# ScalarE takes apart and joins the 16-bit planes of the last four experts' tokens, in place of GpSimd

## The chip, the cores and the metric

The kernel runs on one core of one Trainium2 chip. The metric is the device time of one execution in microseconds (us), of that one core; the times shown are medians over several executions. A core has five engines that run side by side, each through its own queue in order: TensorE (PE in the profile, with its weight loads as PEld), VectorE (DVE), ScalarE (ACT), GpSimd (POOL) and SyncE (SP), which here issues DMAs. An engine waits at the head of its queue until the data of its next instruction are there, and everything behind that instruction waits too.

## The reference, cut to what matters

```python
def _attn_ref(q, k, v):                      # 8 batches, 8 heads, 576 positions, 64 wide
    scores = q @ k^T / 8 + slope[h] * -|i-j|, masked to 0 <= i-j < 128
    return softmax(scores) @ v

def _moe_ref(x, w_gate, w1, w2):             # x: 4608 tokens x 512; 8 experts, 1024 wide
    logits = x @ w_gate                      # 4608 x 8
    cap = 576                                # tokens that one expert may take
    # all (token, expert) pairs in falling order of logit: a token goes to the first
    # expert that still has room
    for e in range(8):
        mask = assigned == e                 # 576 tokens
        out[mask] = relu(x[mask] @ w1[e]) @ w2[e]
```

The output of the attention, as 4608 tokens of 512 float32 numbers, is the input `x` of the mixture of experts. Each of the eight experts gets exactly 576 tokens.

## The kernel before

The first third of the time is the attention (up to about 240 us), which writes `x` to a buffer in HBM and the gate logits to SBUF. It is not touched. Then come the experts, one after the other, in the order in which they fill up. **Round k** (k = 0 to 7) is the work on the k-th expert.

**One round** has two layers. Layer 1 (`layer1`) multiplies the 576 tokens by `w1`: eight blocks f of 128 hidden columns, each 24 matmuls of 288 tokens (192 in all) into two PSUM banks `ph`. ScalarE takes the ReLU out of each bank into `hh` (L1064) and VectorE the remainder into `hlo` (L1069). `ph` has four banks, so that block f+2 needs the banks of block f emptied. Layer 2 (`layer2`) multiplies the result by `w2`: five tiles t of 128 tokens (the last 64), 24 matmuls of 512 columns each for t = 0 to 3 and 16 for t = 4 (112 in all), each tile in one bank `po` out of two. ScalarE copies the bank to `o` (L1094), and GpSimd sends the rows to their places in the output with an indirect DMA (L1099). Float32 operands are used as a sum of two parts, a high part that the matmul takes as it is and a low part that holds the rest; three of the four products are summed. So weights are loaded from HBM by SyncE as `raw` (L958, four buffers), split by ScalarE into the high part of `hl` (L965) and by VectorE into the low part (L967, two instructions each). The tokens' parts are `xh` and `xl`.

**Preparing the next expert's tokens.** During round k the tokens of expert k+1 are gathered by five indirect DMAs (L976, GpSimd, 128 tokens each, the last 64) into `g`, and have to be turned so that the 512 features lie along the partitions. For the experts 1 to 3 TensorE turns them (`turn`). For the experts 4 to 7, that is in the rounds 3 to 6 (`BY_DMA = 3`), a DMA does (`turn_by_dma`), and a DMA transposes only 16-bit elements. So for each of the five tiles:

1. take apart: two copies put the upper and the lower 16 bits of each float32 of `g` into two planes `pl` (L1017);
2. SyncE asks for a transposing DMA from `pl` to `tp` (L1022), behind the loads of that round's weights;
3. join: two copies put the planes of `tp` back as the halves of float32 numbers in `xf` (L1029);
4. ScalarE copies `xf` to `xh` (L1037), and VectorE subtracts to `xl` (L1038).

`g`, `pl`, `tp` and `xf` share a ring of seven buffers (tag `g`), so a tile waits until an earlier one of the ring has been read. In the kernel before, GpSimd does the copies of steps 1 and 3: 20 copies in a round.

**The router** (`Router.phase`) finds the next experts on VectorE in many small instructions, with small matmuls between them on TensorE. Phase p yields the index list of expert p; it runs two rounds ahead, so that phase 5 runs in round 3, phase 6 in round 4 and phase 7 over the rounds 4 and 5. Its last step is a group of 18 matmuls into `m` (L817) that read `loOH` and `mv` (L812, L808, L809). `yield n` in a phase means that it goes on n slots later.

**What sets the order.** `layer1` yields twice per block f and `layer2` three times per tile t, so a round has 31 slots: 0 to 15 in layer 1, 16 to 30 in layer 2. After each, `slot(k, i)` traces what is due: router steps, weight loads (`W_LOAD`), weight splits (`W_SPLIT`), and the steps of the turning (`DMA_AT`: entry n is the slot from which step n is traced). This gives the order of tracing; a scheduler at build time then sets the order on each engine by its own estimate of when operands are ready, so an instruction may stand earlier on an engine that it thinks free. `add_manual_dep(a, b, BEHIND, ...)` puts a behind b in that order and adds no wait.

## Time and profile before

| | us |
|---|---|
| median of three runs (lowest, highest) | 692.59 (692.06, 695.39) |
| the profiled execution's own time | 690.85 |
| its span from first to last instruction | 688.9 |
| attention and the first routing | up to about 240.7 |
| rounds 0, 1, 2 | 240.7 to 416.0 |
| round 3, layer 1 / layer 2 from | 416.0 / 443.8 |
| round 4, layer 1 / layer 2 from | 471.2 / 498.3 |
| round 5, layer 1 / layer 2 from | 526.5 / 553.1 |
| round 6, layer 1 / layer 2 from | 579.5 / 605.1 |
| round 7, layer 1 / layer 2 from | 630.5 / 656.1 |
| last matmul | 681.9 |

Over the span TensorE is busy 95%, VectorE 70%, ScalarE 48%, GpSimd 28%. In a row of instructions of the profile stand the start, the duration, the engine, the line of the kernel, the operation, `out<-in`, the shape, a count, and in square brackets how long the engine sat idle before it and who ended that. A busy TensorE is not yet one at its peak, because matmuls overlap: the distance from one start to the next tells more than the duration.

### The profile page before, as it was taken

The numbers are of one execution on the slowest core, as the hardware profiler recorded it, in microseconds if no ns is written. First come the engines' busy times: TensorE is split into PE (matmuls) and PEld (weight loads), VectorE is DVE, ScalarE is ACT, GpSimd is POOL, SyncE is SP. The second block draws the span as 40 slices with busy tenths as digits, with TensorE's granted clock in tenths as the row PEclk, the third lists the DMA queues.
The fourth block names the chain that finished last, engine by engine and source line by source line (L and its number), as shares of the span: only waits on it lengthen the run. The fifth ranks groups of instructions, "written<-read, shape, count | busy, mean of one in ns | idle before, by whom it ended". The sixth has DMA issues, their size and how long they took to land.

```text
span 688.9 us, 18916 instructions
## 1 busy us (share of the span) xinstructions
PE 657.4 (95%) x7171; PEld 582.2 (85%) x7172; DVE 479.1 (70%) x1985; ACT 332.1 (48%) x991; POOL 192.7 (28%) x376
## 2 busy tenths in 40 slices
PE   7999999999995699999999999999989999999995
PEld 4898998998985399889789779979978978988985
DVE  5788888888887899879669788886775734532310
ACT  6898888888884262334134224324323333432210
POOL 4021221211220301511422017255076075152011
PEclk9999999999997799999999999999999999999998
DMA  8456566566532453615417227635625644621001
GB/s 307 148 181 202 175 193 200 166 211 186 161 106 70 124 191 104 241 39 187 158 36 245 88 92 245 131 106 182 133 98 166 167 111 169 160 52 54 1 25 49
DMA packets 54212, 97.47 MB, mean 141 GB/s; under 512 B 22880, under 2 KB 32224, under 8 KB 54112
## 3 DMA queue, kind: packets, MB, share of 16 engines
q1 hardware_dynamic: 48224, 77.30, 37.0%
q0 software_dynamic: 5888, 18.88, 8.3%
q8 instruction: 58, 0.95, 0.6%
q14 instruction: 42, 0.34, 0.1%
HBM read 72.57 MB, written 18.87 MB: 133 GB/s over the span
## 4 chain that ended last, share of the span: by engine, by line
PE 77%; DVE 12%; DMA 6%; issue 2%; ACT 1%; SPq 1%; POOL 0%; POOLq 0%; DVEq 0%; ACTq 0%
PE ph L1059 20%; PE po L1087 9%; PE po L1088 9%; PE s L54 8%; PE pt L54 7%; PE pt L158 7%; PE po L1090 7%; PE x L54 6%; DMA raw<-in_w_dram 2%; DVE hl L967 2%; DMA tp<-pl 1%; DVE hlo L1069 1%; DMA craw<-in_cst_dram 1%; PE pg L1000 1%; DMA qk<-in_qk_dram 1%
## 5 line engine op out<-in xcount | busy, mean ns | idle before, releaser
L1059 PE MATMUL ph<-xh,hl 128*128 128x288 f32 (+2 forms) x1024 | 188.9, 299 | 0.7 <-DVE lo L534 0.5
L1059 PEld LDWEIGHTS ph<-xh,hl 128*128 128x128 f32 x1024 | 154.7, 189 | 2.4 <-ACT hh L1064 1.0
L145 ACT ACTIVATE u<-u,mn 128x192 f32<-128x192 f32 (+2 forms) x288 | 123.9, 433 | 24.6 <-DVE mn L134 24.5
L1087 PE MATMUL po<-hl,hh 128*128 128x512 f32 (+1 forms) x328 | 128.9, 393 | 0.6 <-ACT o L1094 0.6
L1088 PE MATMUL po<-hl,hh 128*128 128x512 f32 (+1 forms) x328 | 126.4, 385 | 0.0
L967 DVE TENSOR_TENSOR hl<-raw,hl 128x512 fp32r<-128x512 f32 x128 | 88.1, 708 | 48.6 <-ACT hl L965 48.1
L1059 PE MATMUL ph<-xl,hl 128*128 128x288 f32 (+2 forms) x512 | 115.1, 297 | 0.0
L1064 ACT ACTIVATE hh<-ph 128x288 fp32r<-128x288 f32 (+2 forms) x128 | 46.6, 408 | 131.9 <-PE ph L1059 128.8
L134 DVE CUSTOM_DVE_ANT_0 u<-s,bm 128x192 f32<-128x192 f32 x308 | 86.5, 333 | 29.8 <-PE s L54 29.2
L1090 PE MATMUL po<-hl,hlo 128*128 128x512 f32 (+1 forms) x264 | 101.3, 384 | 0.0
L1099 POOL DMA_INDIRECT out_dram<-o,idx x40 | 42.5, 1063 | 153.1 <-ACT o L1094 76.0
L1059 PEld LDWEIGHTS ph<-xl,hl 128*128 128x128 f32 x512 | 84.1, 189 | 0.0
L965 ACT CAST hl<-raw 128x1024 fp32r<-128x1024 f32 x64 | 65.8, 1050 | 25.1 <-DMA raw<-in_w_dram 22.0
L1069 DVE SCALAR_TENSOR_TENSOR hlo<-ph,hh 128x288 fp32r<-128x288 f32 (+2 forms) x128 | 49.4, 417 | 35.8 <-ACT hh L1064 35.1
L1087 PEld LDWEIGHTS po<-hl,hh 128*128 128x128 f32 x328 | 61.8, 188 | 12.3 <-ACT o L1094 1.0
L54 PE MATMUL s<-qk 64*64 64x192 f32 (+1 forms) x1112 | 69.6, 319 | 2.5 <-DVE mn L134 1.8
L1088 PEld LDWEIGHTS po<-hl,hh 128*128 128x128 f32 x328 | 61.8, 188 | 11.0
L1094 ACT COPY o<-po 128x512 f32<-128x512 f32 (+1 forms) x33 | 18.8, 572 | 95.7 <-PE po L1090 77.4
L976 POOL DMA_INDIRECT g<-x,idx x40 | 42.1, 1053 | 72.2 <-issue 31.7
L1090 PEld LDWEIGHTS po<-hl,hlo 128*128 128x128 f32 x264 | 49.6, 188 | 10.0
L158 PE MATMUL pt<-ident_sb,u 128*128 128x128 f32 x368 | 54.2, 282 | 1.4 <-DVE mn L134 1.0
L54 PEld LDWEIGHTS s<-qk 64*64 64x64 f32 x1112 | 48.3, 132 | 8.3 <-issue 2.2
(240 smaller groups left out, 925.8 us busy)
## 6 DMA issues: line engine op xcount, KB each, us to landing
raw<-in_w_dram SPq DMA_DIRECT2D x64, 512.0 KB, 4.4
qk<-in_qk_dram SPq DMA_DIRECT2D x32, 576.0 KB, 4.8
v<-in_v_dram SPq DMA_DIRECT2D x32, 288.0 KB, 3.8
x<-xb SPq DMA_DIRECT2D x14, 512.0 KB, 3.5
x<-xb SPq DMA_DIRECT2D x8, 128.0 KB, 3.3
x<-xb SPq DMA_DIRECT2D x4, 256.0 KB, 2.4
g<-x,idx POOLq DMA_INDIRECT x40, 3.9
out_dram<-o,idx POOLq DMA_INDIRECT x40, 3.2
```

The lines of the kernel that those rows point to most:

```text
L54: put(nc.tensor.matmul(out, w, a, start=start, stop=stop, skip_group_check=True))
L134: put(nc.vector.tensor_tensor_reduce(out=u[rows], in0=x[rows, c:c + 64 * m].rearrange("q (j k) -> q j k", k=64), in1=bm[n % NP][rows, y:y ...
L145: put(nc.scalar.activation(u, u, AF.Exp, bias=st["mn"][:, i:i + 1], scale=-1.0, accum_out=st["sm"][:, i:i + 1]))
L158: put(nc.tensor.transpose(ps[:, c:c + 128], u[:, o + 128 * j:o + 128 * j + 128], ident))
L965: self.last = nc.scalar.copy(hl[:, 0, :], raw)
L967: nc.vector.tensor_tensor(hl[:, 1, c:c + 512], raw[:, c:c + 512], hl[:, 0, c:c + 512].bitcast(F32), ALU.subtract)
L1059: nc.tensor.matmul(pp[t], w[:, a, j, fo:fo + 128], x[:, j, cut[t]:cut[t + 1]], start=(i == 0), stop=(i == 11))
L1064: nc.scalar.activation(o, pp[t], AF.Relu)
L1069: nc.vector.scalar_tensor_tensor(d, pp[t][:, c0:c1], 0.0, o[:, c0:c1].bitcast(F32), ALU.max, ALU.subtract)
L1087: nc.tensor.matmul(out, a, wh, start=(f == 0), stop=False)
L1088: nc.tensor.matmul(out, a, wl, start=False, stop=(f == 7 and t == 4))
L1090: nc.tensor.matmul(out, hl[:, f, 128 * t:128 * t + 128], wh, start=False, stop=(f == 7))
```

## The change

ScalarE does the copies of the steps 1 and 3, 20 in each of the rounds 3 to 6. Two things go with it. The copies are put behind the last layer activation (`self.acted`: the last ReLU, or the last copy of `o`) in the order of ScalarE, and the table `DMA_AT` is new: the steps 1 are due in slots 4 to 8, the transposes in slot 9, and the steps 3, now together with step 4 for each tile, in slots 18, 20, 22, 24 and 26 (the key 2 of the table is not used, since `BY_DMA` stays 3). And the last wait of the router's phases 4 to 7 is one slot longer, as that of the phases 1 to 3 already was. `k > BY_DMA` in the router becomes `k > 3`, which is the same.

```diff
 BY_DMA = 3
-DMA_AT = [0, 1, 1, 2, 2, 2, 7, 7, 7, 7, 7, 9, 9, 10, 10, 10, 17, 19, 21, 23, 25]
+DMA_AT = {2: [10, 11, 11, 12, 12, 12, 13, 13, 13, 13, 13, 23, 24, 25, 26, 27], 3: [0, 4, 5, 6, 7, 8, 9, 9, 9, 9, 9, 18, 20, 22, 24, 26]}
...
-        yield WAITS[6] + (k < 4)
+        yield WAITS[6] + 1
...
+    def behind(self, copy):
+        self.tc.add_manual_dep(copy.ins, self.acted.ins.name, BEHIND, reason="layers first")
+
     def turn_by_dma(self, idx, asked):
...
             for a in range(2):
-                nc.gpsimd.tensor_copy(pl[:r, a, :], words[:r, :, 1 - a])
+                self.behind(nc.scalar.copy(pl[:r, a, :], words[:r, :, 1 - a]))
...
-        for tp, r in tps:
+        xh = self.p["xg"].tile([128, 4, CAP], F32R, name="xh")
+        xl = self.p["xg"].tile([128, 4, CAP], F32R, name="xl")
+        self.xg = xh, xl
+        for h, (tp, r) in enumerate(tps):
             xf = ring.tile([128, 4, 128], F32, name="xf", tag="g")
             words = xf.rearrange("q j t -> q (j t)").bitcast(U16).rearrange("q (j t o) -> q j t o", j=4, o=2)
             for a in range(2):
-                nc.gpsimd.tensor_copy(words[:, :, :r, 1 - a], tp[:, 4 * a:4 * a + 4, :r])
-            xfs.append((xf, r))
-            yield
-        xh = self.p["xg"].tile([128, 4, CAP], F32R, name="xh")
-        xl = self.p["xg"].tile([128, 4, CAP], F32R, name="xl")
-        self.xg = xh, xl
-        for h, (xf, r) in enumerate(xfs):
+                self.behind(nc.scalar.copy(words[:, :, :r, 1 - a], tp[:, 4 * a:4 * a + 4, :r]))
             o = slice(128 * h, 128 * h + r)
             nc.scalar.copy(xh[:, :, o], xf[:, :, :r])
...
-                nc.scalar.activation(o, pp[t], AF.Relu)
+                self.acted = nc.scalar.activation(o, pp[t], AF.Relu)
...
-                    nc.scalar.copy(o[:, cs], po[:, cs])
+                    self.acted = nc.scalar.copy(o[:, cs], po[:, cs])
...
-            while st["made"] < len(DMA_AT) and i >= DMA_AT[st["made"]]:
+            due = DMA_AT[min(k, 3)]
+            while st["made"] < len(due) and i >= due[st["made"]]:
```

How the built order moves is seen at three places. (Line numbers of the changed kernel are up to three higher; its copies are L1020 and L1035.)

**ScalarE, round 5, layer 1.** The round's 16 ReLUs (L1064, two for each block f) with the splits of weights (L965) between them. Before:

```order
L1064 ACTIVATE hh<-ph 128x288 x4
L965 CAST hl<-raw 128x1024
L1064 ACTIVATE hh<-ph 128x288 x4
L965 CAST hl<-raw 128x1024
L1064 ACTIVATE hh<-ph 128x288 x4
```

and with the change:

```order
L1064 ACTIVATE hh<-ph 128x288 x4
L1020 COPY pl<-g 128x512 x2
L965 CAST hl<-raw 128x1024
L1064 ACTIVATE hh<-ph 128x288 x2
L1020 COPY pl<-g 128x512 x4
L1064 ACTIVATE hh<-ph 128x288 x2
L1020 COPY pl<-g 128x512 x2
L1020 COPY pl<-g 64x512 x2
L965 CAST hl<-raw 128x1024
L1064 ACTIVATE hh<-ph 128x288 x4
```

Two copies stand behind the ReLUs of block 1, four behind those of block 2 and four behind those of block 3. The rounds 3, 4 and 6 have the same rows.

**ScalarE, round 5, layer 2.** `o` is the copy of a tile t out of its PSUM bank. Before, the five `xh` stand ahead of all of them:

```order
L1064 ACTIVATE hh<-ph 128x288 x4
L1037 CAST xh<-xf 128x4x128 x4
L1037 CAST xh<-xf 128x4x64
L965 CAST hl<-raw 128x1024
L1094 COPY o<-po 128x512 x4
L965 CAST hl<-raw 128x1024 x4
```

and with the change:

```order
L965 CAST hl<-raw 128x1024
L1094 COPY o<-po 128x512
L1035 COPY xf<-tp 128x512 x3
L1037 CAST xh<-xf 128x4x128
L1035 COPY xf<-tp 128x512
L1037 CAST xh<-xf 128x4x128
L1094 COPY o<-po 128x512
L1035 COPY xf<-tp 128x512 x2
L1037 CAST xh<-xf 128x4x128
L1094 COPY o<-po 128x512
L1035 COPY xf<-tp 128x512 x2
L1035 COPY xf<-tp 128x4x64
```

The joins and the `xh` now stand between the copies of the tiles t = 0 and 1, 1 and 2, 2 and 3, and the split of weights stands ahead of all.

**VectorE, round 4, start of layer 2.** The last VectorE steps of router phase 6 before the matmuls L817, from the remainder of the last block f on. Before:

```order
L1069 SCALAR_TENSOR_TENSOR hh<-ph,hh 128x64
L1038 TENSOR_TENSOR xl<-xf,xh 128x4x128
L847 SCALAR_TENSOR_TENSOR ov<-kmx,ov 128x1
L792 TENSOR_SCALAR hif<-m 128x36
L848 TENSOR_TENSOR flag<-flag,ov 128x1
L500 TENSOR_TENSOR ne<-L_72,b 128x288
L793 TENSOR_SCALAR hif<-hif 128x36
L1038 TENSOR_TENSOR xl<-xf,xh 128x4x128
L795 SCALAR_TENSOR_TENSOR hv<-hif,m 128x72
L800 SCALAR_TENSOR_TENSOR slo<-hif,m 128x72
L797 TENSOR_TENSOR hOH<-c_h_431,hv 128x360
L812 TENSOR_TENSOR loOH<-c_i_429,slo 128x2304
```

and with the change:

```order
L1069 SCALAR_TENSOR_TENSOR hh<-ph,hh 128x64
L847 SCALAR_TENSOR_TENSOR ov<-kmx,ov 128x1
L500 TENSOR_TENSOR ne<-L_72,b 128x288
L848 TENSOR_TENSOR flag<-flag,ov 128x1
L967 TENSOR_TENSOR hl<-raw,hl 128x512
L792 TENSOR_SCALAR hif<-m 128x36
L502 SCALAR_TENSOR_TENSOR cand<-ne,c_eb 128x288
L793 TENSOR_SCALAR hif<-hif 128x36
L967 TENSOR_TENSOR hl<-raw,hl 128x512
L795 SCALAR_TENSOR_TENSOR hv<-hif,m 128x72
L800 SCALAR_TENSOR_TENSOR slo<-hif,m 128x72
L797 TENSOR_TENSOR hOH<-c_h_431,hv 128x360
```

The two `xl` that stood ahead of `loOH` are gone from there (they come behind `mv`), and two low parts of weights and one more router step stand in their place.

On TensorE the only thing that moves is the group L817. In the rounds 3 and 4 it stood behind the 33rd of layer 2's 112 matmuls and stands behind the 42nd; in round 2 it goes from the 90th of layer 2 to the 96th, and in round 5 from the 84th of layer 1's 192 to the 96th. On GpSimd the 80 copies are gone, and nothing but indirect DMAs is left in the rounds 3 to 7: the five gathers for the experts 5, 6 and 7 now stand behind the scatter of tile t = 2 of the rounds 3, 4 and 5 (before, the first four stood behind that of t = 0, t = 0 and t = 4), and those for expert 4 behind that of t = 3 of round 2. The order of SyncE is the same, but for round 5, where a weight load stands behind the second of the five transposes instead of the fourth.

More of the change, by code (lines that the diff above doesn't have):

```diff
@@ L835, in phase @@
             L2 = rt.tile([128, 8, NT], F32, name="L2", bufs=1)
-            eng = nc.vector if k == 0 or k > BY_DMA else self.tc.nc.gpsimd
+            eng = nc.vector if k == 0 or k > 3 else self.tc.nc.gpsimd
             eng.tensor_tensor(L2, L, bc(self.pen.unsqueeze(2), [128, 8, NT]), ALU.add)
-            if k == 0 or k > BY_DMA:
+            if k == 0 or k > 3:
                 nc.vector.scalar_tensor_tensor(self.L1, T1, 100.0 * BIG, L2, ALU.mult, ALU.add)
```

## The prediction

> **What bounds the kernel now.** I read the page first, then TensorE by stretches, then TensorE's starts one by one, and last the two engines that it waits for. In the page, one engine fills the span:
>
> ```profile
> span 688.9 us, 18916 instructions
> PE 657.4 (95%) x7171; PEld 582.2 (85%) x7172; DVE 479.1 (70%) x1985; ACT 332.1 (48%) x991; POOL 192.7 (28%) x376
> ```
>
> So a change to ScalarE and GpSimd can only give what TensorE loses by waiting for them. The view by stretches, here layer 2 of the rounds 3, 4, 5 and 6, shows where that is (after the sum of each stretch: TensorE, weight loads, VectorE, ScalarE, GpSimd, granted clock):
>
> ```profile
> core 0: us, PE busy (x) PEld busy (x) DVE busy (x) ACT busy (x) POOL busy (x), PEclk, DMA share, GB/s
> 443.80:471.17 27.37, 26.28 (x134) 21.44 (x133) 20.81 (x69) 9.20 (x15) 19.42 (x26) 1.00 0.31 102
> 498.25:526.54 28.29, 26.34 (x134) 21.45 (x133) 15.13 (x34) 9.31 (x15) 22.51 (x28) 1.00 0.33 104
> 553.11:579.48 26.37, 25.75 (x115) 20.94 (x113) 7.33 (x13) 9.22 (x15) 20.75 (x27) 1.00 0.35 115
> 605.06:630.47 25.41, 25.41 (x114) 21.03 (x113) 7.43 (x13) 8.80 (x14) 12.05 (x14) 1.00 0.15 48
> ```
>
> The clock is full in all of them, and round 6 has no router, so 25.41 us is the clean length. The others are 1.96, 2.88 and 0.96 longer, part of it router matmuls that stay. What is lost by waiting is read from the starts in the timeline of TensorE, around its three marked idle times in these rounds:
>
> ```profile
> 451.02 0.39 PE L1088 MATMUL po<-hl,hh 128*128 128x512 f32 x1
> 451.24 0.39 PE L1090 MATMUL po<-hl,hlo 128*128 128x512 f32 x1
> 452.72 0.61 PE L817 MATMUL m<-mv,loOH 128*128 128x40 bf16 x18 [1.09 <-DVE mv L809]
> ...
> 505.73 0.39 PE L1090 MATMUL po<-hl,hlo 128*128 128x512 f32 x1
> 508.06 0.61 PE L817 MATMUL m<-mv,loOH 128*128 128x40 bf16 x18 [1.95 <-DVE mv L809]
> ...
> 563.78 0.39 PE L1090 MATMUL po<-hl,hlo 128*128 128x512 f32 x1
> 564.80 0.50 PE L1087 MATMUL po<-hl,hh 128*128 128x512 f32 x1 [0.62 <-ACT o L1094]
> ```
>
> Without a wait one of these matmuls starts 0.23 after the other (25.41 / 112 = 0.227; 451.02 to 451.24). The three steps are 1.48, 2.33 and 1.02, so **1.25 + 2.10 + 0.79 = 4.14 us** is lost. That is all that can be won here; the change has to remove these three and add none.
>
> **The two router waits (1.25 and 2.10).** In the rounds 3 and 4 TensorE stands before L817 until VectorE has written `mv`. The change moves L817 by 9 matmuls, from the 33rd to the 42nd. At 25.41 / 112 = 0.227 each (the clean row above) TensorE gets there 2.04 later. That covers 1.25 wholly, and all but 0.06 of 2.10, if VectorE is not a moment earlier. It is earlier, as its timeline in round 4 shows, between the last remainder of layer 1 and `mv`:
>
> ```profile
> 499.77 0.21 DVE L1069 SCALAR_TENSOR_TENSOR hh<-ph,hh 128x64 fp32r<-128x64 f32 x1
> 500.85 0.69 DVE L1038 TENSOR_TENSOR xl<-xf,xh 128x512 fp32r<-128x512 f32 x1 [0.86 <-ACT xh L1037]
> 501.46 0.67 DVE L847 SCALAR_TENSOR_TENSOR ov<-kmx,ov 128x1 f32<-128x1 f32 x1
> 503.11 0.74 DVE L793 TENSOR_SCALAR hif<-hif 128x36 f32<-128x36 f32 x1
> 503.70 0.68 DVE L1038 TENSOR_TENSOR xl<-xf,xh 128x512 fp32r<-128x512 f32 x1
> 504.31 0.73 DVE L795 SCALAR_TENSOR_TENSOR hv<-hif,m 128x72 bf16<-128x72 f32 x1
> 507.71 0.30 DVE L809 TENSOR_SCALAR mv<-hOH,craw 128x360 bf16<-128x360 bf16 x1
> ```
>
> First, VectorE sits idle 0.86 for an `xh` that waits for a GpSimd copy. Second, two `xl` take 0.61 each, start to start. In their place come two low parts of weights (at most 0.69 each, the same shape) and `cand` (0.45 as a duration). These nearly cancel: -0.86 - 1.22 + 1.38 + 0.45 = -0.25. Third, tiny steps take five times their usual time here. By line, over the whole kernel (lowest, median, highest ns):
>
> ```profile
> L847 DVE SCALAR_TENSOR_TENSOR ov<-kmx,ov x7: 129/148/669, 269.5 to 533.9; 128x1 f32<-128x1 f32 x7
> L793 DVE TENSOR_SCALAR hif<-hif x7: 160/174/742, 271.3 to 535.5; 128x36 f32<-128x36 f32 x7
> ```
>
> The high values are those of the rounds 3 and 4, where GpSimd copies `xf` all through. Back at their medians, the two save 0.52 and 0.57. So `mv` should be 0.25 to 1.3 earlier than at 508.01, and TensorE 2.04 later. Neither wait is left, by either end: **3.35 us**. Behind the moved L817 stands only the index list of the next but one expert, for a gather that now stands behind a scatter 11 us later anyway.
>
> **The wait for `o` (0.79).** Round 5, layer 2, in the timeline of ScalarE:
>
> ```profile
> 555.83 0.62 ACT L1037 CAST xh<-xf 128x512 fp32r<-128x512 f32 x1 [1.95 <-POOL xf L1029]
> 562.91 0.41 ACT L1037 CAST xh<-xf 128x256 fp32r<-128x256 f32 x1 [1.09 <-POOL xf L1029]
> 563.22 1.04 ACT L965 CAST hl<-raw 128x1024 fp32r<-128x1024 f32 x1
> 564.16 1.06 ACT L1094 COPY o<-po 128x512 f32<-128x512 f32 x2
> ```
>
> The bank of tile 0 is full at 553.11 + 24 x 0.227 = 558.6, but its copy stands behind five `xh` that wait for GpSimd's joins, and starts at 564.16. TensorE needs the bank for tile 2. With the change the copy stands ahead of the joins, and this wait goes: **0.79 us**. The joins can then hold up only the copy of tile 1, which has 5.4 us of spare (the bank is wanted a tile later). They are fed in time. In round 5, the tightest, GpSimd's first join was released by the transposes 4.2 before the new place at 558.6:
>
> ```profile
> 554.37 2.26 POOL L1029 COPY xf<-tp 128x512 uint16<-128x512 uint16 x3 [18.40 <-DMA tp<-pl]
> ```
>
> In round 5 a weight load now stands ahead of three of the transposes, and costs ScalarE a microsecond or two of that spare, not TensorE.
>
> **What ScalarE pays.** It gets 80 copies, none of whose kind it does now. The nearest rows, with GpSimd's price for the same copies:
>
> ```profile
> L965 ACT CAST hl<-raw 128x1024 fp32r<-128x1024 f32 x34 | 34.4, 1050 | 1.7 <-PE po L1088 1.7
> L1037 ACT CAST xh<-xf 128x512 fp32r<-128x512 f32 x16 | 9.9, 621 | 18.7 <-POOL xf L1029 18.7
> L806 ACT ACTIVATE mv<-hOH,craw x1: 596/596/596, 229.5 to 229.5; 128x360 bf16<-128x360 bf16 x1
> 578.86 1.99 ACT L965 CAST hl<-raw 128x1024 fp32r<-128x1024 f32 x2
> L1029 POOL COPY xf<-tp 128x512 uint16<-128x512 uint16 x32 | 27.2, 914 | 61.1 <-DMA tp<-pl 60.7
> L1017 POOL COPY pl<-g 128x512 uint16<-128x512 uint16 x32 | 18.8, 628 | 0.2 <-DMA g<-x,idx 0.2
> ```
>
> At the same number of elements a copy is 0.62 (L1037, 4 bytes each); were 16-bit elements twice as dear, 1.05 (L965, twice the elements). Between them lies the only 16-bit row: 596 ns for 360 elements. With the fixed part of 0.19 that L1037 and L965 leave (621 less 512 x 0.84), that is 1.13 ns per element, or 0.77 for 512. I take 0.62, as nearest in shape, and keep 0.77 and 1.05. In a row each costs 0.11 less (two splits in 1.99, not 2.10), so 0.51 to 0.53: say 0.53.
>
> The tight place is layer 1. Round 6, two blocks without router work:
>
> ```profile
> 592.33 0.71 ACT L1064 ACTIVATE hh<-ph 128x288 fp32r<-128x288 f32 x2 [2.49 <-PE ph L1059]
> 595.53 0.71 ACT L1064 ACTIVATE hh<-ph 128x288 fp32r<-128x288 f32 x2 [1.55 <-PE ph L1059]
> 499.11 0.74 DVE L1069 SCALAR_TENSOR_TENSOR hlo<-ph,hh 128x288 fp32r<-128x288 f32 x2
> ```
>
> A block takes 3.20, its two ReLUs 0.71, so 2.49 are free (the split between these two took 0.94 of that). Four copies behind block 2: 4 x 0.53 + 0.11 = 2.23, fits. Four copies and a split behind block 3: 4 x 0.53 + 1.05 = 3.17, so the ReLUs of block 4 are 0.7 late. Their banks are wanted again at block 6, 3.20 after block 4 ends; ReLUs (0.71) and VectorE's remainder (0.74 + 0.14 for the small third) leave 1.6 of spare. So nothing reaches TensorE. With s per copy in a row the lateness is 8s + 1.05 - 4.98, which passes 1.6 at s = 0.69. At 0.77 alone (0.66 in a row) it is 1.35, still inside; at 1.05 (0.94) it is 3.6, and TensorE loses 2.0 in a round. In layer 2 a tile takes 24 x 0.227 = 5.45; the copy of `o`, four joins and two `xh` take 0.59 + 6 x 0.53 = 3.8, and the last `xh` is done 5 us before the next round. **Term: 0, up to 8 where a 16-bit element costs double.**
>
> The Trainium skill bears on that price: "ScalarE: Activation LUTs", section "What ACT_TABLE_LOAD costs", gives 186 ns + 0.833 ns per element for fp32 and bf16 alike, and 93 ns more for a pointer operand. By it the 596 ns above are fixed cost, not a dearer element, and a plain copy is 0.61 (an estimate from that page), which makes the sum the same as mine and the case of a double price unlikely; the 596 ns agree with its 579 to 3%, and no row here shows a plain 16-bit copy.
>
> **GpSimd and SyncE.** The gathers for the experts 5 to 7 now stand behind the scatter of tile 2, that is 3 x 5.45 + 1 = 17.4 us into layer 2, 8 us before the next layer 1. The page has their time from issue to landing:
>
> ```profile
> g<-x,idx POOLq DMA_INDIRECT x40, 3.9
> ```
>
> Five issues of some 1.3 each and 3.9 end 2.4 us into that layer 1; ScalarE's first copy of it comes at 6.4, its last four at 12.8. Free.
>
> **Sum.** 690.85 for the profiled execution less 4.14 is 686.7. The median of the runs shown is 1.74 above that execution, so for a median I forecast 692.59 - 4.1 = **688.5 us**.
>
> **The rivals.** A change of 0.5% (3.46 us) is about what a measurement of this kernel can tell from none.
>
> *Forecast, all three waits go, 688.5:* chance 0.57. For it: the new place of L817 and the new place of `o` each cover their wait without help from anything else. Against it: 4.14 is only 0.7 above the bound.
>
> *A part is given back, 689.2 to 692.6, say 690.5:* chance 0.34. ScalarE's 0.7 us of lateness and VectorE's `xl`, which now wait for a ScalarE that also copies `o`, hold up router steps behind them, and some other small router matmul waits on TensorE in their stead, as L610 and L787 do at times in the rounds 1 and 2. For it: VectorE runs in order and is 15 to 21 us busy of 27. Against it: the `xl` of the rounds 3 and 4 are 11 us ahead of the next router matmul.
>
> *Slower, 695:* chance 0.09. A 16-bit copy costs ScalarE over 0.79 alone, the ReLUs of block 4 come over 1.6 late and TensorE waits for a bank of `ph` in block 6. At 1.05 that is 2.0 in the rounds 5 and 6 and up to that in 3 and 4, 4 to 8 us, say 6.5: 692.6 - 4.1 + 6.5 = 695. For it: GpSimd's joins are 1.4 times as dear as its take-aparts with as many elements, so the form of a 16-bit copy can matter; against it: L1037.
>
> That the change does not do what it says is possible in one way that alters no time: L817's new place alone is worth 3.3 of the 4.1, so the planes may have moved for 0.8.
>
> **How the numbers follow.** Faster by over 0.5%: the forecast, 0.57. Within: 0.34. Slower: 0.09. The range goes from 686.0 (the profiled execution's 686.7, with 0.7 for other steps that a free GpSimd speeds) to 692.0, which takes in nearly all of the second case; the forecast's own is 686.7 to 689.1.
>
> **What would show it.** Right: no idle time of TensorE before L817 in the rounds 3 and 4, nor before L1087 in round 5; layer 2 of round 5 at 25.6 or less, that of 3 and 4 near 26.1; L847 at 0.15 in all rounds; ScalarE's copies at 0.6. Wrong: copies over 0.8 with idle time of TensorE before `ph` of block 6; ScalarE waiting for `tp` for over 5 us; a new wait at L610 or L760.

## The result, and the profile after

| | before | after |
|---|---|---|
| median, us (lowest, highest) | 692.54 (692.06, 695.39) | 685.12 (684.78, 685.35) |
| the profiled execution, its span | 690.85, 688.9 | 684.91, 683.0 |
| first matmul of round 0 / last matmul | 240.7 / 681.9 | 240.2 / 676.9 |

The ratio is 0.9884 (95% interval 0.9857 to 0.9911): 7.4 us by the medians, 5.9 by the two profiled executions. The forecast was 688.5, a ratio of 0.994. Three later takes of the same two kernels, each on a chip of its own, gave 0.9944 (0.9925 to 0.9964), 0.9896 (0.9855 to 0.9937) and 0.9912 (0.9882 to 0.9942), that is 4.5, 6.4 and 7.1 us by the medians. So the change is worth 4 to 7 us, and the first take lies at the upper end; the interval of the smallest take includes the forecast.

The page of the changed kernel, line of the engines:

```profile
PE 656.3 (96%) x7172; PEld 581.8 (85%) x7172; DVE 468.3 (69%) x1985; ACT 375.5 (55%) x1071; POOL 134.4 (20%) x296
```

ScalarE took on 43.4 us and GpSimd gave up 58.3. VectorE, which got and lost next to no work, is busy 10.8 us less. That line already says what the forecast left out.

The view by stretches, with the rounds 3, 4 and 5 (layer 1, layer 2 in turn; the columns as in the prediction):

```profile
416.10:443.20 27.10, 27.10 (x222) 26.57 (x220) 20.94 (x77) 14.28 (x29) 3.89 (x5) 1.00 0.69 190
443.20:469.36 26.16, 26.16 (x134) 21.36 (x133) 17.63 (x68) 15.04 (x25) 8.15 (x9) 1.00 0.43 125
469.36:496.45 27.09, 27.09 (x222) 26.56 (x220) 20.95 (x77) 14.30 (x29) 1.68 (x2) 1.00 0.61 161
496.45:522.64 26.19, 26.19 (x134) 21.36 (x133) 12.78 (x35) 15.04 (x25) 8.13 (x9) 1.00 0.47 131
522.64:549.05 26.41, 26.41 (x215) 26.18 (x214) 19.08 (x59) 14.37 (x29) 2.04 (x2) 1.00 0.63 183
549.05:574.46 25.41, 25.41 (x115) 21.02 (x113) 6.81 (x13) 15.05 (x25) 8.13 (x9) 1.00 0.45 116
```

TensorE is busy all through. Layer 2 of the three rounds lost 1.21, 2.10 and 0.96 us, near the forecast's 1.25, 2.10 and 0.79. But layer 1 of round 3 went from 27.81 to 27.10 too, and that of round 5 from 26.57 to 26.41. Layer 1 of round 3 before, by stretches:

```profile
415.99:443.80 27.81, 27.65 (x222) 26.74 (x220) 23.50 (x75) 9.17 (x19) 12.34 (x18) 1.00 0.76 207
```

Where VectorE writes `mv` and where TensorE reads it, in the timelines of the rounds 3 and 4:

```profile
448.95 0.31 DVE L809 TENSOR_SCALAR mv<-hOH,craw 128x360 bf16<-128x360 bf16 x1
452.91 0.62 PE L817 MATMUL m<-mv,loOH 128*128 128x40 bf16 x18
...
502.43 0.31 DVE L809 TENSOR_SCALAR mv<-hOH,craw 128x360 bf16<-128x360 bf16 x1
506.19 0.62 PE L817 MATMUL m<-mv,loOH 128*128 128x40 bf16 x18
```

Before, `mv` was done 8.86 and 9.76 us behind the first matmul of layer 2 (452.66 less 443.80, 508.01 less 498.25). Now it is 6.06 and 6.29 (449.26 less 443.20, 502.74 less 496.45): 2.8 and 3.5 us earlier, where the forecast had 0.25 to 1.3. TensorE stands at the old place of L817 33 x 0.227 = 7.5 us behind that first matmul. By these rows the new place was not needed; a run below tests it.

The lines of the copies and of two small steps of VectorE (lowest, median, highest ns):

```profile
L1020 ACT COPY pl<-g x40: 621/625/632, 423.2 to 589.5; 128x512 uint16<-128x512 uint16 x32, 64x512 uint16<-64x512 uint16 x8
L1035 ACT COPY xf<-tp x40: 472/766/791, 449.5 to 619.2; 128x512 uint16<-128x512 uint16 x32, 128x256 uint16<-128x256 uint16 x8
L847 DVE SCALAR_TENSOR_TENSOR ov<-kmx,ov x7: 126/148/159, 269.2 to 528.7; 128x1 f32<-128x1 f32 x7
L793 DVE TENSOR_SCALAR hif<-hif x7: 170/173/177, 271.0 to 530.5; 128x36 f32<-128x36 f32 x7
```

Taking apart costs ScalarE 0.63 us (forecast 0.62), joining 0.77 (forecast 0.62, with 0.77 and 1.05 kept as upper bounds), and VectorE's small steps are back at their medians.

### The profile page after: what moved, and what is told of

Its sections match the earlier page's. It is cut to its first block, busy times and chain, and to the rows that moved or that the text cites. A ratio compares the mean times of both kernels' runs of the same rounds, so it can differ in the third digit from the quotient of the medians.

```text
span 683.0 us, 18912 instructions
## 1 busy us (share of the span) xinstructions
PE 656.3 (96%) x7172; PEld 581.8 (85%) x7172; DVE 468.3 (69%) x1985; ACT 375.5 (55%) x1071; POOL 134.4 (20%) x296
## 4 chain that ended last, share of the span: by engine, by line
PE 83%; DVE 11%; DMA 3%; issue 1%; ACT 1%; SPq 0%; POOL 0%; POOLq 0%; DVEq 0%
PE ph L1059 23%; PE po L1087 10%; PE po L1088 10%; PE s L54 9%; PE po L1090 7%; PE pt L54 7%; PE pt L158 7%; PE x L54 6%; DVE hl L967 2%; DMA raw<-in_w_dram 2%; DVE hlo L1069 1%; PE pg L1000 1%; DVE u L134 1%; PE m L610 1%; PE ph L984 1%
## 5 line engine op out<-in xcount | busy, mean ns | idle before, releaser
L1064 ACT ACTIVATE hh<-ph 128x288 fp32r<-128x288 f32 (+2 forms) x128 | 46.7, 409 | 110.5 <-PE ph L1059 107.5
L134 DVE CUSTOM_DVE_ANT_0 u<-s,bm 128x192 f32<-128x192 f32 x308 | 86.5, 333 | 29.8 <-PE s L54 29.2
L967 DVE TENSOR_TENSOR hl<-raw,hl 128x512 fp32r<-128x512 f32 x128 | 85.1, 683 | 24.9 <-ACT hl L965 24.4
L1099 POOL DMA_INDIRECT out_dram<-o,idx x40 | 42.4, 1061 | 279.4 <-ACT o L1094 215.4
L965 ACT CAST hl<-raw 128x1024 fp32r<-128x1024 f32 x64 | 65.9, 1051 | 27.5 <-DMA raw<-in_w_dram 21.6
L145 ACT ACTIVATION_READ_ACCUMULATOR u<-u,mn 128x1 f32 x288 | 54.5, 189 | 0.0
```

Of the source, the lines that this page charges most:

```text
L134: put(nc.vector.tensor_tensor_reduce(out=u[rows], in0=x[rows, c:c + 64 * m].rearrange("q (j k) -> q j k", k=64), in1=bm[n % NP][rows, y:y ...
L145: put(nc.scalar.activation(u, u, AF.Exp, bias=st["mn"][:, i:i + 1], scale=-1.0, accum_out=st["sm"][:, i:i + 1]))
L965: self.last = nc.scalar.copy(hl[:, 0, :], raw)
L967: nc.vector.tensor_tensor(hl[:, 1, c:c + 512], raw[:, c:c + 512], hl[:, 0, c:c + 512].bitcast(F32), ALU.subtract)
L1064: self.acted = nc.scalar.activation(o, pp[t], AF.Relu)
```

## The experiments

All ratios are to the kernel before, on the same chip. The copies are called by what they do: taking apart (L1017, now L1020) and joining (L1029, now L1035).

**The kernel before again.** No edit.

> The kernel before, unchanged, to see how far apart its executions lie. Theory W (waits, and a kernel before whose executions differ): the profiled execution of before, 690.85, was a short one; the kernel before has waits whose length hangs on when the transposing DMAs land, since five xh stand in ScalarE's order ahead of the copies of o. Then its times spread over 1 us or more around 692.5, while those of the changed kernel lay within 0.6 us, and a second profile with a longer time shows more idle time of TensorE than 4.1 + 0.6 in the rounds 3 to 6. Rival B (baseline): the 1.7 us between that execution and the median lie in the attention or in the tail behind the last matmul, and the waits of the rounds 3 to 5 are the same in a second profile within 0.3 us. Ratio to the kernel before: 1.000 +- 0.002 by both.

Measured: 693.03, ratio 1.0003 (0.9977 to 1.0029), from 690.2 to 696.4. The profiled execution (692.84, span 690.8) waited more. Its view of waits (who waits for whom, us in total, times, longest), the two largest rows of the rounds 3 to 5:

```profile
PE m L817 <- DVE mv L809: 3.2, 2, 2.1
PE m L610 <- DVE ind L586: 0.8, 1, 0.8
```

The new one is L610 in round 3; layer 1 of that round took 28.65 us here and 27.81 in the first profile. VectorE and GpSimd ahead of it, in the timeline of this execution:

```profile
424.98 4.08 DVE L967 TENSOR_TENSOR hl<-raw,hl 128x512 fp32r<-128x512 f32 x1
425.12 3.39 POOL L1017 COPY pl<-g 128x512 uint16<-128x512 uint16 x6
```

and in that of the first profile:

```profile
424.80 1.85 DVE L967 TENSOR_TENSOR hl<-raw,hl 128x512 fp32r<-128x512 f32 x1
424.94 1.16 POOL L1017 COPY pl<-g 128x512 uint16<-128x512 uint16 x2
426.27 2.55 POOL L1017 COPY pl<-g 128x512 uint16<-128x512 uint16 x4 [0.17 <-DMA g<-x,idx]
```

The low part of a weight, L967, takes 0.68 us as a rule. Beside a row of six copies it took 4.08, beside a row of two 1.85; in the first profile GpSimd paused for 0.17 us because a gather had not landed, and VectorE came through. So in these two executions the same program lost more or less with the landing of a gather, and the profile on which the sum stood was one of the short ones. The stages of the rounds 3 to 5 add up to 163.49 us in the first profile of before, 164.57 in this one and 158.35 in the changed kernel: 5.1 or 6.2 us, not 4.14. Theory W holds in that a longer execution waits more, with L610 as the part that differs; but the DMA behind it is a gather, where the theory named the transposes. Rival B falls for that part. Other parts of the spread lie ahead of round 0 and behind the last matmul, where both kernels vary: the tail was 6.1 us in one profile of the changed kernel and 7.8 in another.

**L817 later, and nothing else.**

```diff
 (before)
-        yield WAITS[6] + (k < 4)
+        yield WAITS[6] + 1
```

> The kernel before, and of the change only the one longer wait of the router, so that the matmuls into m (L817) stand 9 matmuls later in the rounds 3 and 4; GpSimd still copies. Theory W: in the two rounds mv was written 8.86 and 9.76 us behind the first matmul of layer 2, and TensorE now gets there 42 x 0.227 = 9.5 behind it: the waits 1.25 and 2.10 go but for 0.2 to 0.3. Gain 3.1 to 3.3, median 689.2 to 689.4, ratio 0.9955; the idle time before L1087 in round 5 (0.79 lost) and the late L610 in round 3 (0.6 lost) stay. Rival C (GpSimd's copies slow VectorE, and that is what the change is worth): VectorE runs on at its own slow pace, some other step waits instead, gain under 2, median above 690.5.

Measured: 698.33, ratio 1.0102 (1.0053 to 1.0152): slower. The view of waits, the largest rows:

```profile
PE ph L1059 <- DVE hlo L1069: 2.0, 1, 2.0
PE m L630 <- DVE sat L627: 1.7, 1, 1.7
PE m L786 <- DVE ei L773: 1.5, 1, 1.5
PE m L817 <- DVE mv L809: 1.0, 2, 0.8
```

The waits before L817 fell from 3.0 to 1.0, most of the way to what theory W had (0.2 to 0.3 lost). But the later index list puts all five gathers of round 2 behind the scatter of tile 3, and the copies of round 3 then come as rows of 3 and 7 in place of 4, 2 and 4. For the rounds 4 and 5 the kernel before makes most of its copies in the last 6.3 us of the layer 2 ahead (rows from 465.4 to 470.9 and from 520.3 to 524.8 in its first profile); here they come as two rows of 5, of which the second lies in layer 1. One L967 takes 3.7 us there, and layer 1 of the rounds 3, 4 and 5 takes 29.4, 29.8 and 30.1. Neither theory had that; rival C comes nearest.

**The copies on ScalarE, L817 at its old place.**

```diff
 (after)
-        yield WAITS[6] + 1
+        yield WAITS[6] + (k < 4)
```

> The changed kernel with the matmuls L817 at their old place, behind the 33rd of layer 2. Theory of the prediction (mv only 0.25 to 1.3 us earlier by the move of the copies): L817 waits 0 to 1.0 in round 3 and 0.8 to 1.85 in round 4, so 0.8 to 2.85 us slower than the changed kernel, median 686.0 to 688.0. Theory V (VectorE is faster than that without GpSimd's copies): in the profile of the changed kernel mv is done 6.06 and 6.29 us behind the first matmul of layer 2, and TensorE is at the old place 33 x 0.227 = 7.5 behind it, so there is no wait and the time is that of the changed kernel, 685.1 +- 0.4: the longer wait is worth nothing beside the copies' move.

Measured: 687.15, ratio 0.9916 (0.9887 to 0.9946). The two stretches in question, layer 2 of the rounds 3 and 4:

```profile
446.12:472.29 26.17, 26.17 (x135) 21.37 (x133) 17.70 (x68) 15.04 (x25) 8.16 (x9) 1.00 0.43 125
499.37:525.57 26.20, 26.20 (x135) 21.37 (x133) 12.80 (x35) 15.07 (x25) 8.12 (x9) 1.00 0.45 128
```

They last what they last in the changed kernel, to 0.01 us, and nothing waits before L817. Theory V holds for the waits, where the prediction's theory had 0.8 to 2.85 us of them. By the median alone the two could not be told apart: 687.15 lies in the range of the prediction's theory and not in that of V (685.1 +- 0.4). It is 2 us above the changed kernel's first median but between those of its takes, and the changed kernel was not run beside it. This profile loses its 4 us ahead of round 0 (first matmul at 244.1 in place of 240.2), with a granted clock of 0.91 in its first 60 us, where the changed kernel's has 1.00.

**The new order, with GpSimd copying.**

```diff
 (after)
-                self.behind(nc.scalar.copy(pl[:r, a, :], words[:r, :, 1 - a]))
+                nc.gpsimd.tensor_copy(pl[:r, a, :], words[:r, :, 1 - a])
...
-                self.behind(nc.scalar.copy(words[:, :, :r, 1 - a], tp[:, 4 * a:4 * a + 4, :r]))
+                nc.gpsimd.tensor_copy(words[:, :, :r, 1 - a], tp[:, 4 * a:4 * a + 4, :r])
```

> The changed kernel with the 80 copies back on GpSimd: the new order of the steps (take apart in slots 4 to 8, join in slots 18 to 26, each xh behind its join) and the longer wait stay. Theory of the prediction (order removes the waits, the engine does not matter): L817 and o cost nothing, median 685.1 + 0.6 for the late L610 at most, 685.1 to 686. Theory C (what counts is that GpSimd copies nothing beside VectorE): VectorE's small steps are slow again (L883 and L884 near 0.55 in place of 0.2), waits at L610 or L817 of 0.5 to 2 us come back at other places, and the time is 686.5 to 690. Joins of 0.91 us each on GpSimd, ten in a round, are 9.1 us of 25 and should be done in time by both.

Measured: 700.16, ratio 1.0103 (1.0072 to 1.0135). Layer 2 of the rounds 3 and 4 is as short as in the changed kernel (26.16 and 26.23), but layer 1 takes 34.18, 31.45 and 28.16 us in the rounds 3, 4 and 5. GpSimd and VectorE in the timeline of round 3, layer 1:

```profile
422.21 4.60 DVE L967 TENSOR_TENSOR hl<-raw,hl 128x512 fp32r<-128x512 f32 x1
422.32 3.94 POOL L1020 COPY pl<-g 128x512 uint16<-128x512 uint16 x7
426.84 0.17 DVE L618 TENSOR_TENSOR odd<-m,base 64x8 f32<-64x8 f32 x1
```

L967 stands from just ahead of the row until 0.55 us behind its end. Seven copies of 0.61 each take 3.94 because each starts 0.56 behind the one before: they overlap, without a gap. Behind L967, in VectorE's order, stands what TensorE needs next. Theory C holds in its main point, that what counts is GpSimd's copying beside VectorE, and not in its size (686.5 to 690): small steps are slow again as it had (L847 up to 0.66, L793 up to 0.74), but most of the loss is one large step that stands for a whole row.

**The changed kernel again.** No edit.

> The changed kernel, unchanged, beside the runs below and to be set against the planes alone (687.15). Theory L (lock: a VectorE instruction with two operands in SBUF stands still as long as GpSimd copies without a gap; the changed kernel has no such copies): rounds 3 to 6 last the same as in its first profile to 0.1 us (27.10, 26.16, 27.08, 26.20, 26.40, 25.41, 25.58, 25.41), and what its executions differ by lies ahead of round 0. The median is then 685 to 687, and the later place of L817 is worth nothing beside the move. Rival: it stays at 685.1 +- 0.3, and the 2 us of the run with L817 at its old place are that place's price.

Measured: 689.04, ratio 0.9944. On this chip layer 1 of round 3 took 28.51 us, for a reason told at the end, and that of the rounds 4 to 6 was 0.2 to 0.5 longer; layer 2 of the rounds 3 to 6 is 26.16, 26.20, 25.41 and 25.41 as before. So theory L holds for layer 2 and misses layer 1 and the median (685 to 687). The rival (685.1 +- 0.3) falls, since the changed kernel itself took 689.04 here. That the 2 us above are no price of L817's old place is shown by the profile with that place, whose rounds 3 to 5 take 158.4 us as the changed kernel's do.

**Idle copies on GpSimd.** The changed kernel, with a copy beside each of ScalarE's (the added statement alone; the joins' likewise, in halves):

```diff
 (after)
+                nc.gpsimd.tensor_copy(self.spare[:r], words[:r, :, 1 - a])
```

> The changed kernel, and GpSimd makes the same copies again into a spare tile that nobody reads (the joins in two halves each, since the spare tile holds 256 of their elements): the work is ScalarE's, GpSimd only copies beside it. Theory L: the low parts of the weights (L967, 0.68 us) stand for up to 4 us beside a row of GpSimd's copies, TensorE waits in layer 1 of the rounds 3 to 5 as it did with the order alone (34.2, 31.5 and 28.2 us in place of 27.1, 27.1 and 26.4), 5 to 13 us slower than the changed kernel: 690 to 698. Rival D (dependence: it was the waiting for GpSimd's results, through xh and the ring, that cost): nobody waits for these copies but the ring, 685 to 687.

Measured: 688.38, ratio 0.9932 (0.9906 to 0.9959), beside 689.04 for the changed kernel: no loss by the median, though layer 1 of round 5 takes 27.78 us where the changed kernel has 26.41. GpSimd in the timeline of round 3:

```profile
425.67 5.47 POOL L1020 COPY spare<-g 128x512 uint16<-128x512 uint16 x7
```

and L967 over the whole kernel, by line:

```profile
L967 DVE TENSOR_TENSOR hl<-raw,hl x128: 643/684/1445, 236.4 to 630.3; 128x512 fp32r<-128x512 f32 x128
```

This spoke against theory L as put, and showed what it lacked. All these copies write one spare tile, so each waits for the one before; between two lies a gap of 0.06 us, and the seven take 0.78 each, start to start. VectorE comes in at a gap, L967 takes 1.4 at most, and GpSimd waits in its turn. Two later runs test this by itself.

**One half on ScalarE at a time.** The changed kernel with the joins back on GpSimd, and with the taking apart back on GpSimd (with the new order):

```diff
 (after; joins on GpSimd)
-                self.behind(nc.scalar.copy(words[:, :, :r, 1 - a], tp[:, 4 * a:4 * a + 4, :r]))
+                nc.gpsimd.tensor_copy(words[:, :, :r, 1 - a], tp[:, 4 * a:4 * a + 4, :r])
 (after; taking apart on GpSimd)
-                self.behind(nc.scalar.copy(pl[:r, a, :], words[:r, :, 1 - a]))
+                nc.gpsimd.tensor_copy(pl[:r, a, :], words[:r, :, 1 - a])
```

> Only the taking apart on ScalarE, the joins back on GpSimd (with the new order). Theory L: the loss of the run with all copies on GpSimd lay in layer 1 (7.1, 4.4 and 1.8 us in the rounds 3, 4, 5), beside the take-aparts; without them layer 1 is as in the changed kernel. In layer 2 joins wait for transposes one by one, so that gaps are left: VectorE slower, mv 1 to 3 us later, which the 2 us of L817's later place cover. 0 to 1.5 us slower than the changed kernel, 685.5 to 688. Rival of the prediction (nothing but the three waits in layer 2 matters, so that the joins are what counts): 687 to 689, with waits before L817.

> Only the joins on ScalarE, the taking apart back on GpSimd (with the new order). Theory L: layer 1 loses nearly what it lost with all copies on GpSimd, 8 to 13 us, 693 to 699, with L967 up to 4.6 us and waits before L630, L786 and the remainder L1069; layer 2 stays at 26.2, 26.2 and 25.4. Rival of the prediction (taking apart in layer 1 has cover enough, 0 to 0.7 us): 685 to 687.

Measured: 691.97, ratio 0.998 (0.9962 to 0.9999) with the joins on GpSimd; 704.26, ratio 1.0171 (1.0139 to 1.0204) with the taking apart there. With the joins on GpSimd layer 1 of the rounds 4, 5 and 6 is as in the changed kernel and layer 2 of the rounds 3 to 6 takes 27.83, 27.38, 26.39 and 26.44. Its waits:

```profile
PE m L817 <- DVE mv L809: 2.6, 2, 1.5
PE po L1087 <- ACT o L1094: 1.4, 2, 0.7
```

That is 4.9 us in layer 2 and 2.9 by the medians (689.04 on this chip), more than theory L had (0 to 1.5). The rival had 2 to 4, with waits before L817, and that is what came. They are the forecast's own waits, even with L817 at its late place: in round 3 VectorE stands 2.6 us for an `xh` that waits for a join, and some of its small steps are slow again beside the joins (L793 up to 0.75). With the taking apart on GpSimd it is layer 1: 32.88, 31.96 and 30.99 us in the rounds 4, 5 and 6. VectorE and GpSimd, round 4:

```profile
472.85 4.49 POOL L1020 COPY pl<-g 128x512 uint16<-128x512 uint16 x8
...
473.21 4.67 DVE L967 TENSOR_TENSOR hl<-raw,hl 128x512 fp32r<-128x512 f32 x1
```

The size is beyond theory L's (8 to 13 us; 15.2 over the changed kernel on this chip), the place and the sign are its own. So theory L is right for the taking apart and wrong for the joins, and the two halves pay in two ways: the joins by standing in the way of `o`, `xh` and `mv`, the taking apart by rows that hold VectorE off.

**A gap behind each copy.** The second of these kernels, with a tiny copy that reads the result of each copy and stands ahead of the next:

```diff
 (joins on ScalarE, taking apart on GpSimd)
-                nc.gpsimd.tensor_copy(pl[:r, a, :], words[:r, :, 1 - a])
+                copy = nc.gpsimd.tensor_copy(pl[:r, a, :], words[:r, :, 1 - a])
+                if self.tiny: self.tc.add_manual_dep(copy.ins, self.tiny.ins.name, BEHIND, reason="one by one")
+                self.tiny = nc.gpsimd.tensor_copy(self.spare[:r], pl[:r, a, 0:1])
```

> Joins on ScalarE and taking apart on GpSimd, as in the run that was 1.7% slower than the kernel before (704.26), but behind each of GpSimd's copies stands a copy of one element of its result, for which the next one has to wait, so that there is a gap between two copies. In the slow runs GpSimd's copies followed each other without a gap (0.56 us from start to start at 0.61 long) and a low part of weights on VectorE (L967, 0.68 us) began with the row and ended with it, after 4.6 us; in the run with idle copies each copy waited for the one before, with a gap of 0.06 us, and VectorE came through between them. Theory G (VectorE is held off as long as a row of GpSimd copies has no gap): L967 at most 1.5 us, layer 1 of the rounds 3 to 6 within 1 us of the changed kernel, ratio to the kernel before 0.992 to 0.998. Rival S (what counts is how long GpSimd copies in all): as slow as before or slower, since GpSimd works longer, ratio 1.015 or more.

Measured: 687.49, ratio 0.9932 (0.9905 to 0.9959): 1.7% slower has become 0.7% faster. L967, by line:

```profile
L967 DVE TENSOR_TENSOR hl<-raw,hl x128: 641/684/1447, 237.8 to 629.4; 128x512 fp32r<-128x512 f32 x128
```

and layer 1 of round 4, by stretches:

```profile
472.02:499.07 27.05, 27.05 (x221) 26.55 (x220) 22.72 (x78) 9.17 (x19) 13.09 (x21) 1.00 0.75 179
```

GpSimd was busy 13.09 us in that stretch; in the same stretch without gaps it was 7.29, and TensorE lost 5.8. TensorE, ScalarE and VectorE run their work of the rounds in the same order in both traces. Theory G holds, rival S falls.

**Idle copies without a gap.** The changed kernel, and GpSimd takes apart into two spare tiles in turn (the added statement alone):

```diff
 (after)
+                [nc.gpsimd.tensor_copy(self.spare[q][:r], words[:r, 256 * q:256 * q + 256, 1 - a]) for q in (0, 1)]
```

> The changed kernel, and GpSimd takes the planes apart again into spare tiles that nobody reads, in halves of 256 elements into two spare tiles in turn, so that a copy waits only for the one before the last and the row has no gap. Theory G: VectorE is held off for up to 4 us in layer 1 of the rounds 3 to 6, though nobody waits for these copies; 4 to 14 us slower than the changed kernel, ratio to the kernel before 1.000 to 1.015. Rival D (only who waits for GpSimd's results counts): as the first idle copies, ratio 0.993.

Measured: 697.71, ratio 1.0079 (1.0053 to 1.0106), 12 us over the changed kernel beside it (685.25). Round 5, GpSimd, VectorE and the first wait of TensorE behind them:

```profile
530.94 6.76 POOL L1020 COPY spare<-g 128x256 uint16<-128x256 uint16 x17
...
532.96 5.28 DVE L967 TENSOR_TENSOR hl<-raw,hl 128x512 fp32r<-128x512 f32 x1
...
539.70 0.21 PE L786 MATMUL m<-m,c_low 128*128 128x36 bf16 x1 [3.83 <-DVE ei L773]
```

Nobody reads these copies, and they cost nearly as much as copies that are needed (15 us, above). Theory G holds, rival D falls. The two idle runs leave the order of the other engines as it is in the changed kernel. They differ in more than the gap, since the second copies in halves and leaves the joins out; the cleaner pair is the taking apart on GpSimd without and with the tiny copies.

**The kernel before, with gaps and nothing else** (the same tiny copy behind all 80 of GpSimd's copies):

```diff
 (before)
+    def alone(self, out, source, first):
+        copy = self.nc.gpsimd.tensor_copy(out, source)
+        if self.tiny: self.tc.add_manual_dep(copy.ins, self.tiny.ins.name, BEHIND, reason="one by one")
+        self.tiny = self.nc.gpsimd.tensor_copy(self.spare[:first.shape[0]], first)
...
-                nc.gpsimd.tensor_copy(pl[:r, a, :], words[:r, :, 1 - a])
+                self.alone(pl[:r, a, :], words[:r, :, 1 - a], pl[:r, a, 0:1])
```

> The kernel before, its order and its engines, with a gap behind each of GpSimd's 80 copies (a copy of one element of the result, for which the next one waits). It splits the gain of the change into what the gaps give and what only the move and the new order give. Theory G with order: VectorE gets through, so L967 stays under 1.5 us and the late L610 of round 3 (0.6 to 1.4 lost) goes; but VectorE still sits idle for an xh that waits for GpSimd's joins, which now take 0.1 to 0.3 us longer each, and the copies of o still stand behind five xh, so that 0.8 to 3 us of the 4.1 stay: ratio to the kernel before 0.993 to 0.999. Rival (the lock is all): the waits before L817 go too, ratio 0.990 to 0.993, as fast as the changed kernel. Rival (the place is all): nothing is won, joins later, ratio 1.000 to 1.005.

Measured: 694.19, ratio 1.0027 (1.0007 to 1.0047). Layer 1 of the rounds 3, 4 and 5 is 27.15, 27.05 and 26.41: as in the changed kernel, by gaps alone. The waits that are left (line numbers are five higher here: L1092 is the first matmul of a tile, L1099 the copy of `o`):

```profile
PE po L1092 <- ACT o L1099: 4.7, 4, 2.2
PE m L817 <- DVE mv L809: 1.5, 2, 1.3
```

and layer 1 of round 3 and layer 2 of round 4, by stretches:

```profile
416.82:443.97 27.15, 27.15 (x222) 26.64 (x220) 21.90 (x76) 9.13 (x19) 14.74 (x27) 1.00 0.77 210
498.45:527.65 29.20, 26.64 (x134) 21.36 (x133) 14.09 (x35) 9.22 (x15) 23.89 (x39) 1.00 0.30 98
```

The waits for `mv` fell from 3.0 to 1.5, so about half of them may be VectorE held off; what the other half waits for was not taken apart further, and the joins are nearest. The joins, now slower, hold up `o` for 4.7 us, in the order in which the copies of `o` stand behind the `xh`; the change turns that order round. The ratio is that of the third theory put (the place is all), the parts are nearest the first: gaps win layer 1 and lose more than that in layer 2.

**Expert 3 by DMA too.** The table's entry 2 comes into use; the changed kernel beside it, twice.

```diff
 (after)
-BY_DMA = 3
+BY_DMA = 2
```

> The changed kernel with BY_DMA = 2: expert 3 too is turned by DMA and ScalarE, in round 2, by the table's entry 2, in place of 20 transposes on TensorE. Layer 2 of round 2 is 30.6 us, 4.4 longer than that of round 3, with 59 other matmuls in place of 20; the 20 transposes with their wait (0.6 before L1000) are some 3 us of it. Theory: nothing else comes late, since ScalarE is busy 9 of 30 us there: 2 to 3.5 us faster than the changed kernel. Rival: the copies and transposes of this round are due only from slot 10 on, so that the last xh and xl come late for round 3, or the router's steps in round 2 wait behind xl: 0 to 3 us slower than the changed kernel.

> The changed kernel, unchanged, as a measure for the three runs beside it on the same chip. By every theory its ratio to the kernel before lies between the two taken so far, 0.988 and 0.994; its stages from round 3 on are 27.1, 26.2, 27.1, 26.2, 26.4, 25.4, 25.6 and 25.4 us if TensorE's signals reach ScalarE in time, as they did in its first profile, and some 0.2 to 1.4 us longer in layer 1 if they come late as in the second.

> Expert 3 turned by DMA and ScalarE too, once more, with more executions, beside the changed kernel: in the profile layer 2 of round 2 went from 30.6 to 27.0 and layer 1 of round 3 from 27.2 to 27.6, 3 us in all, while the medians of four executions each differed by 0.7. If the 3 us are there in every execution, its median is 2 to 4 us under that of the changed kernel on the same chip; if the waits of other executions give them back, under 1 us.

> The changed kernel, unchanged, beside the two others on one chip: ratio to the kernel before 0.988 to 0.994 as in the three takes so far.

Measured: 684.53 beside 685.25 (ratios 0.989 and 0.9896), then 683.47 beside 685.51 (0.9878, 0.9852 to 0.9904, and 0.9912, 0.9882 to 0.9942). Layer 2 of round 2 in the second pair, with expert 3 by DMA:

```profile
385.62:412.66 27.04, 27.04 (x145) 21.39 (x144) 21.94 (x99) 14.65 (x25) 4.79 (x5) 1.00 0.44 118
```

and in the changed kernel:

```profile
384.72:415.31 30.59, 30.01 (x173) 23.41 (x172) 23.62 (x102) 9.15 (x15) 6.44 (x6) 1.00 0.22 74
```

The transposes leave TensorE and 3.55 us go with them; layer 1 of round 3 gives 0.58 back (27.68 in place of 27.10). These stages say 3 us, the medians 0.7 and 2.0, at the lower end of what was expected or under it, and the intervals overlap: probably the fastest kernel of all here, not shown to be.

## Why the prediction was right and wrong

- **The three waits** went, as the sum had them: layer 2 of the rounds 3, 4 and 5 is 26.16, 26.19 and 25.41 (forecast near 26.1, 26.1 and at most 25.6). Their size was right, and in part by luck: for two of the three the new place of L817 that the sum counted on was not needed, as the bullets on VectorE and L817 say.
- **"That is all that can be won here"** is the step that failed. The sum held the three idle times marked in one profile. It had no term for layer 1 of the rounds 3 and 5 (0.71 and 0.16 us there), and took the lost time of one execution for that of all: the second profile of before has 6.2 us in the rounds 3 to 5 over the changed kernel, where the first has 5.1 and the sum 4.14. What was missing is that GpSimd's copies hold VectorE off in layer 1 too, there often for a whole row of them. The rows for it were in the prediction (L847 at 669, L793 at 742 ns) and were priced as two slow steps ahead of `mv`, not looked for in layer 1, where L967 at 1.85 was of the same kind; gaps alone take layer 1 of round 3 from 27.81 to 27.15. So 1.0 to 2.1 of the 3.4 us between the forecast and the first median are accounted for. For the rest the runs show no cause in the change; the takes differ by as much (4.5 to 7.4 us).
- **"VectorE is 0.25 to 1.3 earlier"** was 2.8 and 3.5. The count of instructions that leave and come nearly cancelled as it said, but in round 4 seven steps ahead of `mv` were slow, not two: L847, L848, L793, L795, L797, L812 and L808 took 2.9 us longer together than in the changed kernel. L795 at 0.73, against 0.22 there, stands in the prediction's own list.
- **"L817's new place alone is worth 3.3 of the 4.1"** is refuted twice: alone it makes the kernel 1.0% slower, and without it nothing is lost in the rounds 3 to 5. The planes' move with its order, put at 0.8, is nearly all of the gain.
- **The wait for `o`** went for the reason given. In the changed kernel's ScalarE timeline, round 5, it stands ahead of the joins:

```profile
554.71 0.59 ACT L1094 COPY o<-po 128x512 f32<-128x512 f32 x1 [3.96 <-PE po L1090]
555.19 2.03 ACT L1035 COPY xf<-tp 128x512 uint16<-128x512 uint16 x3
```

- **What ScalarE pays** was 0 for TensorE, as forecast: TensorE waits for ScalarE nowhere in the rounds 3 to 6 of the first profile. The joins at 0.77 hit the middle bound, for another reason than the one given (it was the row of 360 elements): the taking apart, with as many 16-bit elements, takes 0.63. One thing that differs is that a join writes every other 16-bit element, where a take-apart reads every other one; GpSimd paid more for a join too (median 770 against some 610 ns alone). No run tests that cause. The 0.61 worked out from the Trainium skill ("ScalarE: Activation LUTs", section "What ACT_TABLE_LOAD costs") agrees with the taking apart, and the trace stands against it for the joins.
- **The rival "a part is given back"** did not come. **The rival "slower"** did not come by its mechanism (a dear ScalarE copy); the prices at which that would begin were not reached.
- **The range** (686.0 to 692.0) missed by 0.9 us at its low end, because the 0.7 us that it had for "other steps that a free GpSimd speeds" had no sum behind them.

## What to carry to other kernels

Before costing a move between engines, look for instructions of a third engine whose longest time is a multiple of their median, and lay the first and the third engine's timelines beside each other there. A step of 0.68 us that becomes 2 to 4 need not show as a marked wait of TensorE, and yet it lengthened a stage by 0.7 to 1.6 us here, and by up to 5.8 where the copies moved. What a row of copies costs hangs on where it lies: a shift of 9 matmuls that covers a wait on paper put rows into layer 1 that had stood at the end of layer 2. After a move, read the order of every engine that shares a resource, not only that of the engine that waits. And one profile's waits are one execution's waits: a second profile of the kernel before would have shown 1.1 us more.

## What the runs showed of the hardware

**VectorE beside GpSimd.** A VectorE instruction with two operands in SBUF and a GpSimd copy did not run side by side here: one of them waited. Beside a row of take-aparts without a gap, L967 mostly stood until the row ended (4.60 us beside 7 copies, 4.67 beside 8, 5.28 beside halves), and where there were gaps of 0.06 us it came in at a gap. This is no rule for every row. In the run with L817 later and nothing else, round 3, it came in while the row went on:

```profile
422.62 2.37 DVE L967 TENSOR_TENSOR hl<-raw,hl 128x512 fp32r<-128x512 f32 x1
422.72 4.86 POOL L1017 COPY pl<-g 128x512 uint16<-128x512 uint16 x7
```

Four L967 did so in that run and in the new order with GpSimd copying. And beside the joins VectorE never stood that long. In round 4 of the first profile of before they make a row without a stop of more than 0.06 us:

```profile
499.40 8.23 POOL L1029 COPY xf<-tp 128x512 uint16<-128x512 uint16 x9
```

Yet the steps of VectorE from 501.46 to 504.31 that the prediction lists came through it one after the other, the small ones some 0.5 us late each, less than one copy takes (median 0.77), and GpSimd's copies were stretched in turn, up to 1.56. What lets VectorE in at one row and not at another is not shown. Some steps with one operand in SBUF are slowed too (L793).

An instruction with an operand in PSUM was not held. In round 3 of the first profile of before the remainders of layer 1 take 0.76 for two in the middle of a row, as they do elsewhere:

```profile
421.13 2.69 POOL L1017 COPY pl<-g 128x512 uint16<-128x512 uint16 x4
423.04 0.76 DVE L1069 SCALAR_TENSOR_TENSOR hlo<-ph,hh 128x288 fp32r<-128x288 f32 x2
```

The Trainium skill, "SBUF — State Buffer", section "Who interferes with whom", states that a VectorE instruction with two SBUF inputs contends with a GpSimd instruction that reads SBUF. Of VectorE's modes that use two ports it says there that whoever issues first gets the shared ports for the whole instruction. The traces agree on who contends; on how long, the rows of take-aparts show more than one instruction: the wait goes on over seven copies of 0.61, each of them finished. How the ports are given out in between was not tried further.

**A stall costs twice.** In layer 1 of round 4 with the taking apart on GpSimd, TensorE was idle for 3.0 us (32.88 less 29.89), and the granted clock of the stretch (the third last number) is 0.90:

```profile
471.02:503.90 32.88, 29.89 (x221) 28.96 (x220) 25.98 (x78) 9.76 (x19) 7.29 (x11) 0.90 0.60 146
```

The stretches of 27 us have 1.00. The same matmuls are busy 29.89 us here and 27.05 with gaps, so that 2.8 of the 5.8 us lost go with the lower clock.

**Late signals.** On the chip of the second take, TensorE's signals reached ScalarE late at a few places in each of the four kernels run there. The first ReLUs of round 3 in that take of the changed kernel:

```profile
423.45 1.32 ACT L1064 ACTIVATE hh<-ph 128x288 fp32r<-128x288 f32 x4 [5.13 <-PE ph L1059]
```

Layer 1 began at 416.97 there, and a matmul takes 25.58 / 192 = 0.133, so block 0 was full at 416.97 + 24 x 0.133 = 420.2; its ReLUs came 3.2 us later, together with those of block 1. In the first profile they came 0.1 us behind it:

```profile
419.36 0.71 ACT L1064 ACTIVATE hh<-ph 128x288 fp32r<-128x288 f32 x2 [1.90 <-PE ph L1059]
```

This made up 1.4 us in that stage, and is part of why that take has the smallest gain (0.9944). The cause stays open.
